# A new order for a fused linear attention and gated MLP kernel, with batch 2's attention output turned by TensorE

## The chip, the cores and the metric

The kernel runs on one core of one Trainium2 chip. The metric is the device time of one execution in microseconds (us), as the median of several runs. The engines are PE (TensorE: matmuls; its weight loads are listed as PEld), DVE (VectorE), ACT (ScalarE), POOL (GpSimd) and SP (SyncE, which here only issues DMAs). Each engine runs its own instructions in the order given, and waits on semaphores where an operand comes from another engine or from a DMA.

## The reference

A linear attention with exponential features, and behind it a gated MLP whose gate mixes the tokens. All inputs are float32, and so is the output (8, 576, 512).

```python
# q, k, v: (8 batches, 8 heads, 576 tokens, 64); w_phi: (64, 128)
def phi(x):
    proj = np.einsum('bhsd,df->bhsf', x, w_phi)
    proj = proj - np.max(np.abs(proj), axis=-1, keepdims=True)
    return np.concatenate([np.exp(proj), np.exp(-proj)], axis=-1)
q_p, k_p = (phi(q), phi(k))
kv = np.einsum('bhsf,bhsd->bhfd', k_p, v)
z = np.sum(k_p, axis=2)
num = np.einsum('bhsf,bhfd->bhsd', q_p, kv)
den = np.einsum('bhsf,bhf->bhs', q_p, z)[..., None] + 1e-06
attn = num / den                       # then heads side by side: x (8, 576, 512)
h = np.maximum(x @ w_in, 0.0)          # w_in: (512, 1024)
u, v = h[..., :512], h[..., 512:]
v_n = (v - mu) / np.sqrt(var + 1e-06)  # over the last axis
v_s = np.einsum('ts,bsd->btd', w_spatial, v_n) + b_spatial[None, :, None]
out = (u * v_s) @ w_out                # w_out: (512, 512)
```

## The kernel before, in words

**Tiles.** A batch has 576 tokens: four chunks of 128 ("main"), and a tail of 64. The tails of two batches share one tile of 128 rows, so there are eight batches (0 to 7) and four tail groups (0 to 3). Work is in bf16, sums in PSUM in float32. PSUM's eight banks are named by hand in each step.

**The order.** Each step is a small function (`@op`). The string ORDER (L17 to L153) lists some 1,500 words, and a loop at the end (L1020) calls one function for each word. A word reads name, arguments, then after a colon the buffer or banks, then after @ the engine where there is a choice: `ckt.1:0@V` is the cast of key tail 1 into buffer 0 on DVE (V; A is ACT, P is POOL, S is SP). The order of the words is the order of the instructions on every engine and DMA queue; nothing reorders them later. The framework puts in the waits that the data and the buffers need.

**The steps of a batch b**, with the names that are used below:
- Loads. `lk`, `lq` load keys and queries with a cast to bf16, issued by POOL (L366, L370); `lv` loads values, `lkt`, `lqt`, `lvt` the tails, issued by SP (L396, L282). Batch 0 is special: its keys come as float32 by SP (`lkf`, L358) and are cast by `ckf`, its queries by `lq0` (L380) on POOL's queue. The weights come on POOL's queue: `lin.0` is w_v, the second half of w_in's columns, `lin.1` is w_u, the first half (L422), `lout` w_out, `lsp` and `lspt` the spatial weights, `lbs` the bias (by SP).
- Turning keys and queries so that the head dimension lies on the partitions: for batches 0 and 1 by PE (`tk`, `tq`, four 128x128 transposes each, L496, with a copy from PSUM `tkc`, `tqc`), for the others by DMA transposes issued by SP (`xk`, `xq`, L482). Tails: cast `ckt`, `cqt`, turned by PE (`tkt`, `tqt`, L524, copies `tktc`, `tqtc`).
- Keys: projection `kp` (L548), maxima `km` (DVE, L553, 1.2 us each), two exponentials `ke` (ACT, L557), the maxima's exponentials `kem`; `vs` scales the values (mostly POOL, L606), `kv` sums over the tokens (L637, L639), `kvc` copies. Tails the same with a t: `kpt`, `kmt`, `ket`, `vst`.
- Queries: `qp`, `qm`, `qs` (split of the maxima), `qt` and `qc` (turned by PE and copied), `qf` (features with the maxima subtracted, L664, L668), `qe` (ACT, L673), `qn` (L720), `qr` and `qx` (division, DVE). Tails again with a t.
- Turning the attention output x: for batches 0, 1 and 7 by PE, `tx` (four transposes, L803) with the copy `txc`; for the others by two DMA transposes `xx` issued by SP (L796). The tails of groups 1 and 2 by the DMA transpose `xxt` (L815), the others by PE (`txt`, L822).
- MLP: `vm` (L835), `vr` (relu), `vb`, `va`, `vx` (DVE statistics), `vw`, `vy`, `vn` (POOL, normalizing), `um` (L931), `ur` (relu), `spt`/`spc` (the spatial weights turned), `sm` (L946, L948), `sg` (gate, DVE), `om` (L960), `oc` (copy), `od` (store by SP). Tails: `vmt`, `umt`, `smt`, `sgt`, `omt`, `oct`, `odt`.
- `warm.n.w` issues n matmuls of w columns on a tile of zeros (L349), whose result nobody reads. They fill places where PE would have nothing to do.

The batches overlap: while one batch is in its MLP, the next ones are at their keys and queries. Buffers are few (3 for `ld`, 7 for the turned T, 4 for v, 2 for the tails' `tf`, 3 for xT), so a load or a transpose can be issued only when the reader of the buffer's last content is through.

Of the kernel before, what the change touches and what calls it, by code (L numbers as in the profile page):

```python
# [33 lines left out]
tkc.1.0.0:4@V kv.0.2:2 qe.0.0.1.0:3 vst.0.1.1@V qet.0.1 kv.0.3:3 qn.0.0.0:0,1 qr.0.0.0:0 qe.0.0.1.1 qf.0.1.1:4,5
kvc.0.2@A kvc.0.3@V qe.0.1.1.0:4 qe.0.1.1.1 qx.0.0.0:0 qn.0.1.0:6,7 lq.2:1 qr.0.1.0:1 qnt.0.0:2,3 qx.0.1.0:1 qrt.0.0:2
qn.0.0.1:0,1 lvt.1:0@S qxt.0.0:0 qr.0.0.1:0 tk.1.0.1:6 spt.4:7 kp.1.0:4,5 tkc.1.0.1@V qn.0.1.1:2,3 qx.0.0.1
warm.1.512:6 warm.1.128:6 tx.0.1:6 tx.0.0:0 spc.4@A ke.1.0.0:4 qr.0.1.1:1 qx.0.1.1 txt.0.0:1 txc.0.0:0@A txtc.0.0:0@V
# [5 lines left out]
va.0.1 kp.1.2:4,5 ur.0.0:1@A ke.1.2.0:1 vs.1.0.0:0@P qp.1.0.1:0,1 vsz.1.1@P vxt.0.0 vx.0.0 spt.3:3 qm.1.0.0:1 vb.0.2:3
qm.1.0.1:2 ke.1.2.1 vs.1.0.1@P um.0.3:2 vwt.0.0:0 kp.1.3:6,7 um.0.1:0 vb.0.3:0 ur.0.3@A va.0.2:2 xk.2.0:3 vw.0.0:1
va.0.3 ke.1.3.0:2 ke.1.3.1 vsz.1.0@P lv.2.0:1@S kv.1.0:1 spc.3@V um.0.2:2 vx.0.1 lout spt.2:3 km.1.2:3 kvc.1.0:1@A
qp.1.1.0:4,5 qs.1.0.0:2@P km.1.3:0 warm.2.128:3 spt.0:1 vy.0.0 warm.5.128:1 qt.1.0.0:6 qs.1.0.1:0@P vyt.0.0 spc.2@A
ur.0.1@A kem.1.3:2 qt.1.0.1:0 kv.1.1:3 tkt.1:7 qm.1.1.0:3 vw.0.1:2 vn.0.0:1@P qp.1.1.1:4,5 qc.1.0.1:1@V vy.0.1
qc.1.0.0:0@V vnt.0.0:0@P vn.0.1@P spc.0@A kvc.1.1@V vn.0.3@P vn.0.2@P lk.3:0 xk.2.1:4 qm.1.1.1:0 vs.1.3.0:2@P
qf.1.0.0:0,1 qs.1.1.0:1@P vs.1.3.1@P cqt.1:0@A warm.2.128:3 sm.0.2:3 sm.0.3:6 qe.1.0.0.0:1 ur.0.2@A qe.1.0.0.1
qf.1.0.1:4,5 kem.1.2:3 sg.0.2 qp.2.1.0:2,3 qp.2.0.0:0,1 vsz.1.3@P tktc.1:0@A sg.0.3 lv.3.1:2@S qm.2.1.0:1 sm.0.0:6  # L50
sm.0.1:7 qt.1.1.0:2 vs.1.2.0:3@P qm.2.0.0:2 qe.1.0.1.0:0 qs.1.1.1:2@P lkt.2:0@S vsz.1.2@P vs.1.2.1@P qc.1.1.0:2@V
qt.1.1.1:3 qe.1.0.1.1 xk.3.0:5 sg.0.1 qc.1.1.1:0@V kv.1.3:4 qn.1.0.0:0,1 sg.0.0 kvc.1.3@A qr.1.0.0:2 kv.1.2:2
qx.1.0.0:2 qf.1.1.0:4,5 qp.2.0.1:6,7 kvc.1.2@A qnt.0.1:2,3 qe.1.1.0.0:3 qn.1.0.1:0,1 qm.2.0.1:3 qrt.0.1:0 warm.2.128:1
qf.1.1.1:6,7 qxt.0.1 qr.1.0.1:1 qe.1.1.0.1 warm.2.128:1 txt.0.1:2 qx.1.0.1 txtc.0.1@V qp.2.1.1:4,5 lq.3:1 qe.1.1.1.0:4
qm.2.1.1:0 xk.3.1:2 om.0.3:3 qn.1.1.0:0,1 qe.1.1.1.1 tx.1.0:2 qn.1.1.1:6,7 oc.0.3:0@A xq.3.0:0 qr.1.1.0:2 qx.1.1.0:0
tx.1.1:3 kpt.1:4,5 qr.1.1.1:0 qx.1.1.1 kp.2.0:0,1 txc.1.0:1@A txc.1.1@A ke.2.0.0:3 vmt.0.1:2 qs.2.0.1:0@P kmt.1:1
vrt.0.1:0@A vm.1.0:3 ket.1.0:0 tx.1.3:2 km.2.0:2 tx.1.2:6 vm.1.1:7 txc.1.3@V vm.1.3:2 vr.1.0:1@A qs.2.1.0:1@P
kem.2.0:0 vbt.0.1:2 txc.1.2@V qt.2.1.0:3 vr.1.1:2@V qs.2.0.0:2@P om.0.0:6 vat.0.1:3 vxt.0.1 ket.1.1 lk.4:2 ke.2.0.1
tqt.1:7 vs.2.0.0:0@P vr.1.3:4@A tqtc.1:0@A vb.1.0:1 kp.2.1:4,5 kp.2.2:0,1 va.1.0:4 vm.1.2:2 qc.2.1.0:1@V vs.2.0.1@P
vb.1.1:3 ke.2.1.0:4 umt.0:3 kemt.1:1 va.1.1 vwt.0.1:3 vr.1.2:3@A om.0.2:7 oc.0.0:1@A vb.1.3:0 vx.1.0 um.1.0:2  # L60
urt.0:0@A km.2.1:0 qt.2.0.0:3 km.2.2:3 vb.1.2:2 va.1.2:5 um.1.2:6 qc.2.0.0:2@V va.1.3 ke.2.1.1 kem.2.1:2 qf.2.1.0:4,5
vyt.0.1 um.1.3:3 vx.1.1 oc.0.2:2@A ke.2.2.0:0 ur.1.0:2@V qe.2.1.0.0:1 kem.2.2:3 xq.3.1:3 qt.2.0.1:2 om.0.1:7 ur.1.2@V
smt.0.0:6 vnt.0.1@P vw.1.0:4 qs.2.1.1:1@P qc.2.0.1:0@V ur.1.3@V vy.1.0 oc.0.1:3@V qe.2.1.0.1 sgt.0.0 vn.1.0:2@P
kp.2.3:2,3 ke.2.2.1 vs.2.1.0:1@P qf.2.0.0:4,5 kp.3.0:6,7 qt.2.1.1:0 vw.1.1:0 vn.1.1@P vy.1.1 km.2.3:2 vst.1.0.0:0@P
um.1.1:1 qc.2.1.1:1@V vn.1.3@P vn.1.2@P qe.2.0.0.0:2 od.0.2@S sm.1.2:0 vs.2.1.1@P lv.3.0:3@S qe.2.0.0.1 km.3.0:1
xk.4.0:4 od.0.3@S ur.1.1@A qp.3.0.0:4,5 lv.4.1:1@S lq.5:0 smt.0.1:1 ke.2.3.0:2 sg.1.2 sm.1.0:0 qm.3.0.0:3 vsz.2.0@P
sgt.0.1 ke.2.3.1 vst.1.0.1@P qp.3.0.1:4,5 od.0.0@S ke.3.0.0:1 sm.1.1:1 vstz.1@P sg.1.0 vs.2.2.0:2@P vsz.2.1@P
kem.2.3:0 ke.3.0.1 qf.2.0.1:2,3 qs.3.0.0:2@P qe.2.0.1.0:0 qm.3.0.1:1 qpt.1:4,5 sg.1.1 qmt.1:2 kp.3.1:6,7 sm.1.3:0
vs.2.3.0:3@P xk.4.1:6 qe.2.0.1.1 kv.2.0:1 vs.2.2.1@P kv.2.1:4 km.3.1:0 omt.0:5 sg.1.3 ckt.2:0@A ke.3.1.0:3 kem.3.1:2
kvc.2.0:2@V vsz.2.2@P vs.2.3.1@P oct.0:4@A vst.1.1.1@P kp.3.3:2,3 kvc.2.1@V km.3.3:3 ke.3.1.1 qp.3.1.1:0,1 vsz.2.3@P  # L70
kv.2.2:4 kv.2.3:5 kvc.2.2@A qm.3.1.1:0 kem.3.0:3 qn.2.0.0:6,7 kvc.2.3@A qr.2.0.0:1 ke.3.3.0:4 qx.2.0.0:1 warm.1.128:4
qn.2.0.1:4,5 od.0.1@S om.1.3:0 qr.2.0.1:2 qf.2.1.1:6,7 vst.1.1.0@P kem.3.3:0 qx.2.0.1 qp.3.1.0:4,5 ke.3.3.1 qm.3.1.0:3
# [983 lines left out]
```

## Time and profile before

| | |
|---|---|
| median of 3 runs | 266.23 us (264.95 to 268.85) |
| the profiled execution | 265.98 us, of which its span is 264.2 us |
| granted TensorE clock | 0.999 |
| PE's matmuls on zeros (L349) | 19.1 us busy |
| DMA | 41.91 MB, 159 GB/s on average |
| queue of SP and queue of POOL | 56.3% and 29.0% of 16 engines' span |
| keys, queries: issue to landing (median) | 7.8 and 8.9 us |
| values: least, median, most | 4.2, 7.3, 18.3 us |
| DMA transposes T<-ld (24), xT<-x (10), xTt<-xt (2), median | 5.5, 4.4 and 5.2 us |

How to read it: the span is the time from the first to the last instruction in the profile, and what is predicted is the device time. Busy time of an engine is the sum over its instructions; matmuls overlap in the pipeline, so their spacing in a row is shorter than the duration of one. An idle time is put down to what ended it. A share of the DMA above 1 in a stretch means that the transfers' packets overlap.

The first PE work on data starts 4.1 us into the span (`tk.0.0.0`), the first `kv` at 24.5, the first `vm` at 36.5, the first `um` at 44.6, the first `om` at 65.9 us. The last `kv` runs to 221 us; from there on only the MLPs of batches 5 to 7 and the last queries are left. The last matmul starts at 259.6 us; the last copy and store end the span.

### The profile page before, as it was taken

How to read it: one execution, taken by the hardware profiler on the slowest of the kernel's cores; microseconds unless marked ns; L12 is line 12 of the kernel's file. 1: busy time of each engine (PE TensorE's matmuls, PEld its weight loads, DVE VectorE, ACT ScalarE, POOL GpSimd, SP SyncE). 2: the span in 40 equal slices, each digit the busy share in tenths (PEclk: the TensorE clock that was granted, in tenths of full speed). 3: DMA queues.
4: the chain of work that ended last, by engine and by line, in shares of the span. 5: the costliest groups of instructions: out<-in, count | busy, mean ns of one | idle time of the engine just before them, and what ended most of it. 6: DMA issues, size and time to landing. Idle time of an engine off the chain costs nothing.

```text
span 264.2 us, 8269 instructions
## 1 busy us (share of the span) xinstructions
PE 249.1 (94%) x3305; PEld 152.4 (58%) x3342; DVE 219.8 (83%) x438; ACT 203.7 (77%) x338; POOL 164.1 (62%) x297
## 2 busy tenths in 40 slices
...
GB/s 150 219 204 252 204 221 230 194 238 179 166 61 194 181 120 125 157 175 182 227 159 246 275 90 180 141 178 188 201 78 2 123 122 2 0 110 51 122 186 213
DMA packets 82075, 41.91 MB, mean 159 GB/s; under 512 B 50994, under 2 KB 77298, under 8 KB 82036
## 3 DMA queue, kind: packets, MB, share of 16 engines
q1 hardware_dynamic: 64612, 31.28, 56.3%
q0 software_dynamic: 17424, 10.10, 29.0%
...
## 4 chain that ended last, share of the span: by engine, by line
PE 69%; DVE 11%; DMA 7%; issue 4%; POOL 3%; SPq 2%; ACT 2%; POOLq 0%; ACTq 0%; DVEq 0%
PE banks L946 9%; PE banks L960 9%; PE banks L931 8%; PE banks L835 8%; PE banks L637 6%; PE banks L548 5%; PE banks L720 5%; DMA xT<-x 3%; PE banks L664 3%; DMA xTt<-xt 2%; DVE mq L553 2%; PE banks L349 2%; PE banks L948 2%; PE banks L668 2%; DMA ob<-in_k_dram 2%
## 5 line engine op out<-in xcount | busy, mean ns | idle before, releaser
L673 ACT ACTIVATE qf<-banks 128x1024 bf16<-128x1024 f32 x72 | 70.4, 1033 | 4.9 <-PE banks L668 4.6
L606 POOL TENSOR_TENSOR vs<-v,em 128x512 bf16<-128x512 f32 x59 | 60.8, 1040 | 20.7 <-ACT em L563 7.6
L557 ACT ACTIVATE kf<-banks 128x1024 bf16<-128x1024 f32 x64 | 64.7, 1036 | 3.3 <-PE banks L548 2.1
L553 DVE TENSOR_REDUCE mq<-banks 128x8 f32<-128x1024 f32 x36 | 43.4, 1216 | 2.3 <-PE banks L548 1.9
L553 DVE TENSOR_REDUCE mk<-banks 128x8 f32<-128x1024 f32 x36 | 43.4, 1214 | 1.8 <-PE banks L548 1.1
L844 POOL TENSOR_TENSOR rs<-mv,neghalf 128x2 f32<-128x2 f32 (+2 forms) x21 | 13.9, 664 | 32.2 <-DVE mv L841 26.4
L835 PE MATMUL banks<-w_v,xT 128*128 128x512 bf16 x116 | 30.7, 380 | 2.7 <-DMA xT<-x 2.1
L946 PE MATMUL banks<-w_spT,vn 128*128 128x512 bf16 x121 | 32.1, 380 | 0.5 <-issue 0.2
L931 PE MATMUL banks<-xT,w_u 128*128 128x512 bf16 x128 | 32.3, 380 | 0.0
L960 PE MATMUL banks<-w_out,uT 128*128 128x512 bf16 x116 | 30.9, 380 | 0.8 <-issue 0.2
L548 PE MATMUL banks<-wphi,T 64*128 64x128 bf16 x512 | 24.3, 218 | 1.6 <-DVE T L268 1.1
L850 POOL TENSOR_SCALAR vn<-vr,rs,mv 128x512 bf16<-128x512 bf16 x31 | 23.5, 764 | 0.7
L637 PE MATMUL banks<-vs,kf 128*128 128x66 bf16 x512 | 23.8, 194 | 0.0
L637 PEld LDWEIGHTS <-kf 128*128 128x128 bf16 x512 | 21.8, 98 | 3.3 <-issue 0.5
L955 DVE TENSOR_TENSOR uT<-banks,uT 128x512 bf16<-128x512 f32 x32 | 21.2, 679 | 2.6 <-PE banks L948 1.8
L733 DVE TENSOR_TENSOR x<-banks,rc 128x512 bf16<-128x512 f32 x32 | 21.9, 686 | 1.1 <-PE banks L349 0.4
L862 DVE BATCH_NORM_STATS2 st<-vr 128x6 f32<-128x512 bf16 x32 | 21.6, 677 | 0.9 <-ACT vr L272 0.8
L548 PEld LDWEIGHTS <-T 64*128 64x128 bf16 x512 | 15.7, 94 | 10.7 <-issue 7.8
L272 ACT ACTIVATE vr<-banks 128x512 bf16<-128x512 f32 (+1 forms) x26 | 15.7, 605 | 7.9 <-PE banks L835 4.8
L349 PE MATMUL banks<-blank 128*128 128x128 bf16 (+1 forms) x96 | 19.1, 315 | 2.6 <-DVE blank L344 1.2
L720 PE MATMUL banks<-kv,qf 128*128 128x66 bf16 x512 | 21.1, 194 | 0.0
L639 PE MATMUL banks<-vst,kft 128*128 128x66 bf16 x128 | 21.0, 192 | 0.0
...
## 6 DMA issues: line engine op xcount, KB each, us to landing
...
```

Of the source, the lines that this page charges most:

```text
L349: nc.tensor.matmul(out=bank(place)[:, 512 - w:512], lhsT=blank[:, 0:P], rhs=blank[:, 0:w], start=True, stop=True)
L548: nc.tensor.matmul(out=bank(banks[y])[:, n * F:(n + 1) * F], lhsT=xT[halves[y], n, :], rhs=wphi[halves[y], :], start=True, stop=True)
L553: nc.vector.tensor_reduce(out=out_, in_=pp.rearrange("p y (n f) -> p y n f", f=F), axis=AX.X, op=ALU.max, apply_absolute_value=True)
L557: nc.scalar.activation(out=kf[:, s].rearrange("p y n f -> p y (n f)"), in_=pp, func=AF.Exp, bias=0.0, scale=(1.0, -1.0)[s])
L606: ENG[e].tensor_tensor(out=at["vs", (b, j)][:, s, :, 0:D], in0=at["v", (b, j // 2)][:, (j % 2) * n:(j % 2 + 1) * n, :], in1=at["em", (b, j ...
L637: nc.tensor.matmul(out=pv[:, hh, s, :], lhsT=kf[:, s, c % 2, 2 * hh + c // 2, :], rhs=w[:, s, NB * hh + c, :], start=(c == 0), stop=False)
L673: nc.scalar.activation(out=at["qf", u][:, s].rearrange("p y n t -> p y (n t)"), in_=at["pq", u], func=AF.Exp, bias=0.0, scale=(1.0, -1.0)[s])
L720: nc.tensor.matmul(out=at["pn", u][:, y, n, :], lhsT=f[:, s, y, n, :], rhs=at["kv", b][:, hg * HH + n, s, :], start=(s == 0), stop=(s == 1))
L835: nc.tensor.matmul(out=bank(place)[r], lhsT=lhs[:, kc, r], rhs=w_v[:, kc, :], start=(kc == 0), stop=(kc == KC - 1))
L931: nc.tensor.matmul(out=bank(place).rearrange("p (c t) -> p c t", c=NB), lhsT=w_u[:, kc, dc * P:(dc + 1) * P], rhs=at["xT", b][:, :, kc, :] ...
L946: nc.tensor.matmul(out=bank(place), lhsT=at["vn", b][:, c, cs], rhs=w_spT[:, c, 0:T0], start=(c == 0), stop=False)
L960: nc.tensor.matmul(out=bank(place), lhsT=at["uT", b][:, dc, c * P:(c + 1) * P], rhs=w_out[:, dc, :], start=(dc == 0), stop=(dc == KC - 1))
```

## The change

Only ORDER changes; every function stays as it is.

- `xx.2.0` and `xx.2.1` go; `tx.2.0` to `tx.2.3` and `txc.2.0` to `txc.2.3` come in (16 transposes on PE, three copies on DVE, one on ACT).
- `lin.0` stands behind `lk.1` (the second batch's keys) and `lsp` in POOL's queue; `lspt` is POOL's first word, and `lq.1` and `lin.1` come much earlier. On SP the loads `lkf.3`, `lv.3.0`, `lqt.3` come earlier, `lv.1.0`, `lv.2.1`, `lkt.3` later.
- Nearly all other words stand in another place, and some change engine: `ckf` from two on ACT, one each on POOL and DVE to three on POOL, one on DVE; `ckt` from three on DVE, one on ACT to two on POOL, one each on ACT and DVE; `cqt` from one to three of four on POOL; `tkc` from five to seven of eight on DVE; `ur` from 20 to 26 of 32 on ACT; `vr` from 22 to 18 of 32 on ACT; `kvc` from 14 to 16 and `oc` from 16 to 14 of 32 on DVE; `vn` from 31 to 29 on POOL, the others on DVE.
- The matmuls on zeros go from 49 of 512 columns and 51 of 128 columns to 39 and 32.

The diff replaces the whole string; here are its start and the lines that hold the words spoken of.

```diff
-zblank@V zmhl.2@V zmhl.1@V zmhl.0@V lkf.0:0,0@S cident csel chalf@P ckf.0@A lphi@S zvnt.1@A zvnt.0@V warm.8.512:0
-tk.0.0.0:0 zsp@V lkf.1:1@S lkf.2:2@S cphi@V ckf.1@P warm.4.512:1 warm.2.128:1 tk.0.0.1:1 lkt.0:0@S tkc.0.0.0:0@A
-tkc.0.0.1@V ckf.2@A lq0.0.4:1 warm.3.512:0 kp.0.1:2,3 tk.0.1.0:0 km.0.1:0 tkc.0.1.0:1@A ckt.0:0@V lq0.4.4 kp.0.0:4,5
-lqt.0:1@S csel2@V ke.0.0.0:0 warm.2.512:1 warm.1.128:1 kp.0.2:6,7 lkf.3:3@S km.0.2:1 kem.0.1:0 ke.0.0.1 ckf.3@V
-lv.0.0:0@S km.0.0:2 warm.1.512:0 warm.3.128:0 tkt.0:0 tktc.0:0@A ke.0.1.0:1 lin.0 cqt.0:0@P warm.7.512:1 warm.1.128:1
-tk.0.1.1:0 warm.4.512:1 kpt.0:4,5 ke.0.1.1 tqt.0:1 kem.0.2:1 zvst.0@V ke.0.2.0:2 warm.2.512:2 warm.1.128:2 tq.0.0.1:2
-tq.0.0.0:3 kmt.0:3 tkc.0.1.1@V tqc.0.0.0:2@A tqtc.0:0@V tqc.0.0.1@V warm.1.512:0 warm.1.128:0 qpt.0:0,1 ke.0.2.1
-qmt.0:0 warm.1.512:3 qp.0.1.0:2,3 kem.0.0:2 ket.0.0:0 lk.1:2 qm.0.1.0:1 warm.2.512:6 warm.1.128:6 tq.0.1.1:6
-tq.0.1.0:7 kp.0.3:0,1 kemt.0:3 tqc.0.1.0:3@V qs.0.1.0:0@V lspt:4 lsp:0 vs.0.1.0:0@P ket.0.1 qst.0:1@P lvt.0:0@S
+lkf.0:0,0@S zblank@V lphi@S lkf.1:1@S lkf.2:2@S lspt:3 cident zmhl.1@V zvnt.0@A ckf.1@P ckf.0@V zmhl.2@V warm.7.512:0
+warm.2.128:0 tk.0.0.0:0 csel warm.7.512:1 warm.2.128:1 tk.0.0.1:1 lkt.0:0@S zmhl.0@V tkc.0.0.0:0@V zvst.0@V lq0.0.4:1
+lq0.4.4 lk.1:2 zvnt.1@V cphi@V warm.1.512:0 warm.2.128:0 kp.0.0:2,3 km.0.0:0 tkc.0.0.1@V ckt.0:0@P ke.0.0.0:0
+lkf.3:4@S ckf.2@P warm.8.512:0 warm.1.128:0 kp.0.1:4,5 warm.1.512:0 warm.1.128:0 tkt.0:0 kem.0.0:0 lqt.0:1@S
+warm.1.512:1 tk.0.1.0:1 tktc.0:0@A lsp:0 ke.0.0.1 lin.0 ckf.3@P lv.0.0:0@S csel2@V km.0.1:1 tkc.0.1.0:1@V cqt.0:0@P
+warm.1.512:6 warm.2.128:6 kpt.0:6,7 kmt.0:2 kp.0.2:0,1 ke.0.1.0:1 km.0.2:3 ke.0.1.1 kem.0.1:1 warm.3.512:2
+warm.3.128:2 tk.0.1.1:2 warm.1.512:3 tqt.0:3 warm.6.128:2 tq.0.0.0:4 tkc.0.1.1@V lq.1:0 tq.0.0.1:5 tqc.0.0.0:2@V
+tqtc.0:0@A lvt.0:0@S ket.0.0:0 tqc.0.0.1@V qpt.0:2,3 qmt.0:0 warm.1.512:4 warm.2.128:4 qp.0.1.0:4,5 ke.0.2.0:2
+qm.0.1.0:1 ket.0.1 qp.0.0.0:2,3 kp.0.3:6,7 qs.0.1.0:0@P qst.0:1@P tq.0.1.0:4 warm.1.512:5 warm.2.128:5 qt.0.1.0:5
...
-ke.0.3.1 warm.2.512:3 warm.2.128:3 kv.0.0:0 lq.1:0 lv.1.0:2@S lbs:0@S vs.0.2.1@V kem.0.3:2 qe.0.0.0.0:1 qt.0.0.1:1
-qc.0.1.1:2@V warm.2.512:0 warm.1.128:0 tk.1.0.0:0 vs.0.3.1@V qet.0.0:2 vsz.0.3@P lin.1 vst.0.1.0@P kvc.0.1@V
+lin.1 qm.0.0.0:2 ke.0.2.1 tq.0.1.1:0 vs.0.1.0:0@P qs.0.0.0:2@V tqc.0.1.0:3@A tqc.0.1.1@V qc.0.1.0:0@A ke.0.3.0:3
...
-xq.2.1:1 va.0.0:0 vm.0.3:1 vs.1.1.0:1@P warm.1.512:4 tq.1.0.1:6 tq.1.1.1:4 ckt.1:0@V vr.0.2:3@A vat.0.0:1
+kem.1.0:1 kem.1.1:0 spb@P vr.0.1:1@A lk.2:2 chalf@P lout ke.1.0.1 vb.0.0:0 ckt.1:0@P tx.0.3:4 spt.3:2 vr.0.2:2@A
...
-qs.3.0.1:0@P kp.3.2:2,3 xx.2.0:2 om.1.2:1 lq.4:1 qst.1:1@P qt.3.0.0:4 om.1.1:5 km.3.2:2 xq.5.1:5 vs.3.0.0:0@P
-qx.2.1.0:2 qn.2.1.1:4,5 kv.3.0:6 qr.2.1.1:1 kp.4.0:2,3 qx.2.1.1 xx.2.1 vs.3.2.0:3@P vs.3.3.1@P vsz.3.3@P kvc.3.0:0@V
+qe.2.1.1.0:3 om.1.2:7 kem.3.3:0 qe.2.1.1.1 qtt.1:2 km.3.2:0 om.1.1:3 oc.1.3:1@V tx.2.1:6 ke.3.2.1 oc.1.2:4@V
+qf.3.0.0:4,5 qe.3.0.0.0:4 oc.1.1:2@V tx.2.0:7 qn.2.1.0:0,1 qs.3.1.1:0@P od.0.3@S qct.1:2@V qe.3.0.0.1 vs.3.0.1@P
+qs.3.1.0:2@P qn.2.1.1:2,3 txc.2.0:2@V vs.3.3.0:2@P om.1.0:7 vsz.3.0@P qr.2.1.0:0 vst.1.1.0@P txc.2.1@V vs.3.3.1@P
+kv.3.2:1 kvc.3.2@A kem.4.0:1 tx.2.3:2 qf.3.1.0:4,5 qe.3.0.1.1 qnt.1.2:0,1 txc.2.3@V va.2.1 qrt.1.2:2 xq.4.0:0
+qxt.1.2:0 qn.3.0.0:2,3 qn.3.0.1:6,7 qr.3.0.0:0 vm.2.3:0 qx.3.0.0:1 tx.2.2:1 qe.3.1.0.0:0 vx.2.0 xxt.1:1 qe.3.1.0.1
+qr.3.0.1:1 txc.2.2@A qx.3.0.1 xx.3.0:0 qf.3.1.1:2,3 kp.4.1:4,5 lk.5:2 qn.3.1.0:6,7 vm.2.2:1 qe.3.1.1.0:3 vr.2.3:0@V
...
-qr.3.0.0:0 qe.3.0.1.1 qx.3.0.0:0 qt.3.1.1:7 qc.3.1.1:0@V qn.3.0.1:4,5 qe.3.1.0.0:1 vr.2.2:2@A vm.2.3:2 xxt.1:1
-um.3.0:2 od.1.2@S ke.5.0.0:3 va.3.0:3 lvt.2:0@S vr.3.3:1@A lkt.3:0@S sg.2.3 ke.5.0.1 qt.4.0.1:0 vr.3.2:4@V va.3.1
-ke.4.3.0:0 qp.5.1.1:0,1 qs.4.1.1:1@P kem.4.3:3 sg.3.1 qm.5.1.1:2 ckt.3:0@V ke.4.3.1 qf.4.0.0:4,5 qf.4.1.0:6,7 sm.3.2:2
+qx.4.1.0:1 kp.5.3:0,1 qe.5.0.1.0:3 lk.7:2 qmt.2:3 om.3.0:4 om.3.3:5 qe.5.0.1.1 lkt.3:1@S km.5.3:0 ckt.3:0@V qt.5.1.0:2
```

237 lines of the change are left out of this document (118 added, 119 removed).

## The prediction, made before the changed kernel was run

> **What bounds the kernel now.** I read the page's busy shares first, then a table of busy time by stretches of 8 us (busy us and instruction count of PE, PEld, DVE, ACT, POOL; granted clock; DMA share; GB/s), then the same table for the fill matmuls of L349 alone, and last the timelines around PE's waits.
>
> ```profile
> PE 249.1 (94%) x3305; PEld 152.4 (58%) x3342; DVE 219.8 (83%) x438; ACT 203.7 (77%) x338; POOL 164.1 (62%) x297
> ```
>
> ```profile
> 0.00:8.00 8.00, 6.47 (x41) 2.88 (x43) 3.00 (x12) 4.05 (x7) 3.15 (x11) 1.00 0.65 165
> 8.00:16.00 8.00, 6.77 (x69) 3.58 (x68) 7.22 (x11) 6.83 (x13) 3.71 (x6) 1.00 1.15 209
> 16.00:24.00 8.00, 7.67 (x107) 4.68 (x108) 7.52 (x10) 7.19 (x14) 6.00 (x13) 1.00 1.25 235
> ...
> 40.00:48.00 8.00, 6.85 (x75) 3.85 (x73) 7.78 (x18) 7.05 (x12) 6.45 (x13) 1.00 1.28 206
> ...
> 104.00:112.00 8.00, 6.10 (x133) 4.40 (x128) 4.62 (x9) 6.14 (x9) 4.76 (x10) 1.00 1.09 157
> 112.00:120.00 8.00, 6.93 (x105) 4.07 (x101) 7.51 (x22) 7.32 (x9) 1.13 (x4) 1.00 1.40 175
> ...
> 128.00:136.00 8.00, 7.95 (x51) 3.70 (x51) 7.97 (x16) 4.91 (x11) 5.35 (x12) 1.00 0.98 172
> ...
> 256.00:264.00 8.00, 3.90 (x18) 1.56 (x16) 0.05 (x1) 3.17 (x6) 0.00 (x0) 0.99 0.53 199
> ```
>
> And the fills alone (PE busy, PEld busy, clock, DMA):
>
> ```profile
> 0.00:8.00 8.00, 5.46 (x17) 1.81 (x17) 1.00 0.65 165
> 8.00:16.00 8.00, 4.82 (x23) 2.01 (x24) 1.00 1.15 209
> 16.00:24.00 8.00, 4.26 (x28) 2.04 (x29) 1.00 1.25 235
> ```
>
> PE is 94% busy, but 14.5 us of its first 24 us are fills: of 20.9 us busy there only 6.4 us is work, and the start is set by loads and by DVE. From 24 to 120 us PE stands idle 6.1 us (8.00 less its busy time, stretch by stretch); after 120 us nearly nothing until the last output leaves. So what is saved ahead of 120 us reaches the end, if DVE allows it: it too is 97 to 99% busy in several stretches. PE's timeline shows where the idle time lies:
>
> ```profile
> 44.27 0.40 PE L548 MATMUL banks<-wphi,T 64*128 64x128 bf16 x8 [1.15 <-DVE T L268]
> ...
> 106.31 0.81 PE L835 MATMUL banks<-w_v,xT 128*128 128x512 bf16 x3 [1.90 <-DMA xT<-x]
> ...
> 119.93 1.04 PE L835 MATMUL banks<-w_v,xTt 128*128 128x512 bf16 x3 [0.98 <-DMA xTt<-xt]
> ```
>
> **Batch 2 turned by PE.** Gone are two DMA transposes (xx.2.0, xx.2.1) and the 1.90 us for which vm.2.0 waited on the first, which took 8.0 us to land. Added are 16 transposes; eight of L803 stand in a row as 0.61 us, so 16 cost 1.2 us of PE. The four copies (three on DVE at 0.42, one on ACT at 0.59) lie where DVE has 3.4 us free (104 to 112 us); without that cover they cost DVE 1.2 us. Net -0.7; bounds -0.7 and, if the next transposes are late instead, +1.2.
>
> **The tail's transpose.** xxt.1 cost 0.98 us: it took 6.5 us to land. Between its source qxt.1.2 and its reader vmt.1.2 the changed order puts one um (0.86) and one qn (0.51) more, two groups of four transposes more (0.3 each) and one qf less (0.5): about 1.2 us more of cover. I take -0.98; bounds -0.98 and 0. For xxt.2 the cover falls by one um, from about 5.0 to 4.2 us of PE work, against 3.8 us to land: 0, at worst +0.8.
>
> **The cast ckt.1.** The 1.15 us before 44.27 trace back to DVE, where one cast took four times its usual time while POOL multiplied:
>
> ```profile
> 42.07 1.75 DVE L268 CAST tl<-tf 128x512 bf16<-128x512 f32 x1
> ```
>
> ```profile
> 42.49 1.04 POOL L606 TENSOR_TENSOR vs<-v,em 128x512 bf16<-128x512 f32 x1
> ```
>
> The cast of the same shape at 147.30 us, with POOL empty, took 0.42 us. The change puts ckt.1 on POOL (0.61 us there), in front of two vs multiplications that have slack. -1.15; bounds -1.15 and 0. The Trainium skill (SBUF — State Buffer, "SBUF: two separate sides") says that POOL and a DVE cast in a two-port mode share a port pair by an exclusive lock, whoever starts second waiting it out; the row agrees. By that rule ckt.3, still on DVE and now among POOL's vs, could pay the same 1.33 us, and the sum below would be 1.3 us higher.
>
> **Fills.** Of 512 columns there are 39 for 49, of 128 columns 32 for 51. Eight wide ones in a row take 1.73 us, eight narrow ones 0.62, so 0.216 and 0.078 each. Ahead of kv.0.0 (24.5 us) go 7 wide and 3 narrow (1.75 us), behind it 3 and 16 (1.9 us). A fill that goes is worth something only if no wait takes its place. Behind kv.0.0 I take half, -0.95; bounds -1.9 and 0.
>
> **The start.** Casts move to POOL: there ckf.1 (ends at 6.19), two lq0 issues (0.99, 0.76), lk.1 (0.9), ckt.0 and ckf.2 (0.61 each) now stand in a row, so ckf.2 ends near 10.1 us against 6.83 on ACT, and tk.0.1.0 waits for it. In return kp.0.0 and kpt.0 go first, and DVE clears the vst and vnt blocks earlier. The queries' load still lands at 14.5 us (PE waited for it there), the first values at 15.4. I take 0; bounds -1.75 (the fills) and +1.2 (one DVE maximum later).
>
> **Weights and loads.** lin.0 moves behind lk.1 and lsp in POOL's DMA queue, lq.1 and lin.1 forward from 25 us to some 13 us. Before, w_v landed at 20.1 us and was read at 36.5; the spatial weights, last of the queue's first loads, landed at 29.7. Now w_v comes last of the same loads, so near 29.7: about 6 us of cover are left, and I cost it at 0. Beyond 6 us late, each us costs one. On SP, lkt.3 now comes closer to ckt.3 (11.6 us of PE work instead of 15 us); its kind lands in 6.8 us (median), 15.3 at most: 0, at worst +3.7, with all of DVE's queue behind the cast.
>
> **DVE's share.** Ahead of om.2.3 (136 us) DVE has 4.1 us more: five more oc (0.68), four txc, two tkc, two tktc, one ur and one qm, less four kvc, two ckt, two txtc, a vr and a vs. ACT has 3.9 us less. DVE stood idle about 11 us between 24 and 136 us, a third of it in the stall at 104 that goes, so most of it fits: +0.6; bounds 0 and +4.1.
>
> Sum: -0.7 - 0.98 - 1.15 - 0.95 + 0.6 = -3.2 us on 264.2, so a span of 261.0. The profiled run took 265.98 us, 1.8 more than its span, and the median of the runs is 0.25 above it: 263.0 us.
>
> **Rivals.** (a) Everything fits: the start gives up its 1.75 us of fills, the rest all 1.9, DVE costs nothing: -6.5, span 257.7, 259.7 us. For it: the fills stand where PE would have idled, and fewer are needed. Against it: DVE, not PE, is full from 8 to 24 us. (b) DVE becomes the bound between 60 and 140 us: PE's gains only turn into waits for DVE, and its extra 4.1 us count in full: span 268.3, 270.3 us. It decides if DVE still idles more than 4 us between 24 and 136 us (11, less 4.1, less the 3.2 forecast): then its extra work no longer fits. For it: 7.97 of 8.00 at 128. Against it: the idle at 104 goes. (c) The loads brought forward, 1.0 MB of lq.1 and lin.1, at 209 to 235 GB/s 4.5 us of transfer, get ahead of the values, which already took up to 14 us to land: 265.5, 267.5 us. Against it: POOL's queue was never empty until 29.7 us anyway. The Trainium skill (DMA: Bandwidth & Descriptors, "Issuing engines are not separate DMA queues") says that loads of SP and POOL interleave on the same 16 engines; the DMA shares above 1.00 agree, and it speaks for (c). (d) The stall moves: the next transposes (xx.3, xxt.1) are late in place of xx.2, and only ckt.1's gain stands against 1.2 us of transposes: 264.2, 266.2 us.
>
> **Numbers.** Forecast 0.36, (a) 0.27, (b) 0.20, (c) 0.10, (d) 0.07. A change under 2% (5.3 us) is about what a measurement of this kernel cannot tell from none. Faster by more, below 260.9: (a) and a quarter of the forecast's spread, 0.36. Slower by more, above 271.6: half of (b), where the cast or a late tail load adds to it, part of (c) and the forecast's upper end: 0.16. The rest 0.48. The range runs from 257.5, (a) with part of PE's unnamed 2 us of idle time, to 270.5, just above (b); the forecast's own is 260 to 266.
>
> **What would show it.** No wait of L835 on xT<-x near 100 us and 16 more transposes of L803; no cast of tl over 0.7 us; vmt.1.2 without a wait; PE's fills in the first 24 us near 12.8 instead of 14.5 us with kv.0.0 near 24.5 us; DVE busy 7.8 or more from 60 to 140 us without PE waiting on it. I am wrong if PE's idle time between 24 and 120 us stays near 6 us, or if POOL waits long for v.

## The result and the profile after

The changed kernel takes 269.04 us (median of 20 runs, 267.77 to 270.36), the kernel before in the same series 266.52 us (20 runs): a ratio of 1.0105, 95% interval 1.0081 to 1.0128. It became slower by 1%, where the forecast had 1.2% faster. Medians here and below are over all runs, while the ratios leave out runs in a slower state that the chip is in at times (three of the twelve of "start freed" below). The profiled execution took 268.97 us with a span of 267.2, against 264.2 before.

From the page after, the busy line and the granted clock in 40 slices:

```profile
PE 248.6 (93%) x3292; PEld 153.0 (57%) x3329; DVE 223.3 (84%) x439; ACT 201.7 (75%) x336; POOL 167.3 (63%) x302
...
PEclk9996899999999999999999999999999999999998
```

DVE has 3.5 us more and ACT 2.0 less than before, in the direction in which the order moved words. New is the clock: the fourth and fifth slice (20 to 33 us) show 6 and 8 tenths. The table by stretches of 8 us of the changed kernel (busy us and count of PE, PEld, DVE, ACT, POOL; granted clock; DMA share; GB/s):

```profile
0.00:8.00 8.00, 6.28 (x29) 2.98 (x29) 3.62 (x12) 2.42 (x3) 3.59 (x9) 1.00 0.68 179
8.00:16.00 8.00, 7.57 (x95) 4.98 (x95) 7.15 (x11) 5.95 (x11) 6.41 (x10) 1.00 1.22 218
16.00:24.00 8.00, 3.56 (x52) 2.17 (x51) 7.93 (x7) 5.78 (x11) 4.50 (x8) 0.90 1.20 222
24.00:32.00 8.00, 7.63 (x121) 5.50 (x121) 7.42 (x15) 6.47 (x12) 4.17 (x11) 0.68 1.29 195
...
104.00:112.00 8.00, 7.90 (x152) 5.58 (x153) 7.56 (x17) 7.59 (x12) 6.70 (x11) 1.00 0.81 105
112.00:120.00 8.00, 7.95 (x170) 5.82 (x168) 7.13 (x19) 7.50 (x13) 2.88 (x6) 1.00 0.85 103
128.00:136.00 8.00, 7.95 (x64) 3.93 (x66) 7.35 (x11) 5.15 (x8) 4.79 (x8) 1.00 1.24 194
```

From 104 to 120 us PE is full where it had been idle for 3 us: what the change was forecast to win there arrived. The largest loss stands in one stretch, 16 to 24 us: PE is busy 3.56 of 8 us (7.67 before), while DVE shows 7.93 with only 7 instructions. From the start of the span to the last matmul, PE's idle time in its timelines is:

| PE idle, us | 0 to 24 | 24 to 120 | behind 120 |
|---|---|---|---|
| before | 3.1 | 6.1 | 1.7 |
| changed | 6.6 | 2.9 | 4.1 |
| changed, `qs.0.0.0` on POOL (below) | 5.1 | 3.1 | 1.9 |

So the 3.2 us less between 24 and 120 us is outweighed by 3.5 us more at the start and 2.4 us more behind 120. The fills of L349 alone, again in stretches of 8 us (PE busy, clock, DMA share, GB/s), are 12.5 us in the first 24, where 14.5 stood before:

```profile
0.00:8.00 8.00, 5.82 (x21) 1.00 0.68 179
8.00:16.00 8.00, 5.26 (x31) 1.00 1.22 218
16.00:24.00 8.00, 1.42 (x9) 0.90 1.20 222
```

The timelines of DVE, POOL and PE in the changed kernel (start, us, engine, line, operation; in brackets the idle time before it and who ended it) say why:

```profile
19.16 0.80 POOL L422 DMA_DIRECT2D w_u<-in_moe_w_in_dram  x1
19.42 3.63 DVE L654 CAST mhl<-mq 128x8 bf16<-128x8 f32 x1
19.98 2.05 POOL L606 TENSOR_TENSOR vs<-v,em 128x512 bf16<-128x512 f32 x2
21.98 1.04 POOL L619 TENSOR_TENSOR vst<-vt,em 64x512 bf16<-64x512 f32 x1
23.17 0.42 DVE L268 COPY T<-banks 128x512 bf16<-128x512 bf16 x1
23.65 0.40 PE L548 MATMUL banks<-wphi,T 64*128 64x128 bf16 x4 [3.26 <-DVE T L268]
...
178.75 1.04 PE L835 MATMUL banks<-w_v,xTt 128*128 128x512 bf16 x3 [1.07 <-DMA xTt<-xt]
```

A cast of 128x8 numbers, `qs.0.0.0`, which the change moved from POOL to DVE, takes 3.63 us; a cast of the same line and shape takes 0.15 at 28.10 us. It starts while POOL issues a DMA and ends when the third POOL multiplication ends that follows without a gap. Behind it in DVE's queue waits the copy `tqc.0.1.1`, and PE waits 3.26 us for that. The first `kv` starts at 29.0 us, not 24.5. (The last line, at 178.75 us, is a wait for a DMA transpose that comes up again below.)

How the lag runs on is estimated from the traces: the time at which PE had done the same amount of listed work (each matmul group at its undisturbed duration, fills left out; the changed kernel has 0.9 us more of it, the 16 transposes, which count from about 110 us on).

| work done, us | 8 | 20 | 76 | 83 | 132 | 160 | 223 |
|---|---|---|---|---|---|---|---|
| before | 25.2 | 39.8 | 100.0 | 109.5 | 160.7 | 189.3 | 252.9 |
| changed | 29.1 | 43.7 | 102.8 | 110.2 | 160.8 | 190.8 | 254.3 |
| changed, qs.0.0.0 on POOL (below) | 25.6 | 40.8 | 99.9 | 107.3 | 157.4 | 187.1 | 250.6 |

So against the kernel before the changed one starts 4 us late, has made good all but about 1 us of that at 160 us (0.1 us by the table and the 0.9 us of transposes), then loses 1.4 us again by 191 us and keeps that lag to 254. Behind its last matmul it loses another 0.8: from there to the end of the span it is 5.0 us, against 4.2 before. Against the same order with `qs.0.0.0` on POOL, the third row, it is 2.9 to 3.7 us late all the way.

### The profile page after: what moved, and what is told of

It reads as the page before. It is cut to its first block, busy times and chain, and to the rows that moved or that the text cites. A ratio compares the mean times of both kernels' runs of the same rounds, so it can differ in the third digit from the quotient of the medians.

```text
span 267.2 us, 8261 instructions
## 1 busy us (share of the span) xinstructions
PE 248.6 (93%) x3292; PEld 153.0 (57%) x3329; DVE 223.3 (84%) x439; ACT 201.7 (75%) x336; POOL 167.3 (63%) x302
## 4 chain that ended last, share of the span: by engine, by line
PE 71%; DVE 13%; DMA 6%; ACT 4%; issue 2%; SPq 1%; POOL 1%; DVEq 0%; ACTq 0%
PE banks L946 10%; PE banks L835 9%; PE banks L931 8%; PE banks L960 8%; PE banks L637 6%; PE banks L548 6%; PE banks L720 4%; PE banks L664 3%; DMA xT<-x 3%; PE banks L948 3%; PE banks L668 2%; DMA xTt<-xt 2%; DVE mq L553 2%; PE banks L349 2%; PE banks L639 1%
## 5 line engine op out<-in xcount | busy, mean ns | idle before, releaser
L606 POOL TENSOR_TENSOR vs<-v,em 128x512 bf16<-128x512 f32 x60 | 61.7, 1040 | 8.0 <-ACT em L563 5.6
L960 PE MATMUL banks<-w_out,uT 128*128 128x512 bf16 x117 | 30.1, 379 | 0.9 <-DVE x L733 0.2
L272 ACT ACTIVATE uT<-banks 128x512 bf16<-128x512 f32 x26 | 15.7, 610 | 11.9 <-PE banks L931 11.8
L548 PEld LDWEIGHTS <-T 64*128 64x128 bf16 x512 | 15.8, 95 | 14.3 <-issue 9.3
L850 POOL TENSOR_SCALAR vn<-vr,rs,mv 128x512 bf16<-128x512 bf16 x29 | 22.0, 767 | 0.8
L720 PEld LDWEIGHTS <-qf 128*128 128x128 bf16 x512 | 18.8, 98 | 3.2 <-issue 0.3
```

The source lines that it names most:

```text
L548: nc.tensor.matmul(out=bank(banks[y])[:, n * F:(n + 1) * F], lhsT=xT[halves[y], n, :], rhs=wphi[halves[y], :], start=True, stop=True)
L606: ENG[e].tensor_tensor(out=at["vs", (b, j)][:, s, :, 0:D], in0=at["v", (b, j // 2)][:, (j % 2) * n:(j % 2 + 1) * n, :], in1=at["em", (b, j ...
L720: nc.tensor.matmul(out=at["pn", u][:, y, n, :], lhsT=f[:, s, y, n, :], rhs=at["kv", b][:, hg * HH + n, s, :], start=(s == 0), stop=(s == 1))
L960: nc.tensor.matmul(out=bank(place), lhsT=at["uT", b][:, dc, c * P:(c + 1) * P], rhs=w_out[:, dc, :], start=(dc == 0), stop=(dc == KC - 1))
```

## The experiments

Theory 1: the cast is kept out while POOL works back to back, and this sets the end. Theory 2: the late start is made good anyway, and the loss comes behind 150 us. Theory 3: it is the place in DVE's queue, not POOL's work. Each ratio is to the kernel before, run on the same chip.

| kernel | median, us | ratio [95%] |
|---|---|---|
| changed, other form of the cast | 268.90 | 1.0105 [1.0059, 1.0151] |
| changed, qs.0.0.0 on POOL | 266.42 | 1.0009 [0.9971, 1.0047] |
| changed, one multiplication in the way, not three | 267.03 | 1.0056 [1.0017, 1.0095] |
| changed, PE's wait filled | 268.83 | 1.0095 [1.0059, 1.0131] |
| qs.0.0.0 on POOL, batch 2 by DMA | 269.69 | 1.0170 [1.0108, 1.0231] |
| qs.0.0.0 on POOL, vmt.2.2 later | 266.77 | 1.0013 [0.9974, 1.0052] |
| that, and ckf.1 on ACT | 271.33 | 1.0213 [1.0155, 1.0271] |
| qs.0.0.0 and ckt.3 on POOL | 265.79 | 0.9986 [0.9950, 1.0022] |
| that, vmt.2.2 later ("late part") | 265.59 | 0.9999 [0.9966, 1.0032] |
| qs.0.0.0 on POOL, start freed | 266.81 | 0.9992 [0.9953, 1.0031] |
| late part and start freed | 267.02 | 1.0046 [1.0011, 1.0080] |
| late part, vm.3 later | 267.65 | 1.0062 [1.0033, 1.0092] |
| before, ckt.1 on POOL | 266.65 | 1.0013 [0.9975, 1.0052] |
| before, batch 2 by PE | 267.10 | 1.0068 [1.0031, 1.0106] |
| before, both of these | 266.68 | 1.0021 [0.9994, 1.0047] |

### The long cast: form, place, and POOL's work

Another form of instruction, in the same place:

```diff
-        ENG[e].tensor_copy(out=m[:, :, 0:HH], in_=mq)
+        if e == "V":
+            nc.vector.tensor_tensor(out=m[:, :, 0:HH], in0=mq, in1=mq, op=ALU.max)
+        else:
+            ENG[e].tensor_copy(out=m[:, :, 0:HH], in_=mq)
```

> The changed kernel, where DVE rounds the maxima to bf16 by a TENSOR_TENSOR (max of mq with itself) instead of a CAST; same place, same queue, same values. Theory 1 (the CAST of qs.0.0.0, 3.63 us at 19.42, was kept out by POOL's back-to-back work; other DVE TENSOR_TENSORs of SBUF ran 0.68 us beside such POOL work): the rounding takes about 0.2 us, PE's wait of 3.26 us at 23.65 is gone, the granted clock of 16 to 32 us is 1.00 again, and the time falls by 3 to 4 us, to about 265.5. Theory 2 (the late start is made good before 125 us anyway, and the loss is in waits after 150 us): the cast and the wait go, but the time falls by less than 1 us, to 268 or more. Theory 3 (the wait is not the cast's own form, but its place in DVE's queue behind data that POOL makes): the rounding still ends near 23 us, no gain.

Nothing changed. DVE's and POOL's timelines of this kernel:

```profile
19.91 3.63 DVE L655 TENSOR_TENSOR mhl<-mq 128x8 bf16<-128x8 f32 x1
...
20.47 2.05 POOL L606 TENSOR_TENSOR vs<-v,em 128x512 bf16<-128x512 f32 x2
22.47 1.03 POOL L619 TENSOR_TENSOR vst<-vt,em 64x512 bf16<-64x512 f32 x1
```

By its letter this is what theory 3 expected. What it refutes is only the belief that a TENSOR_TENSOR goes free: it too ends with POOL's third operation. The Trainium skill (SBUF — State Buffer, "Who interferes with whom") says that a DVE instruction with two inputs in SBUF contends with a GpSimd instruction that reads SBUF; this run agrees, and the expectation had overlooked it. Two runs with the form left alone part theory 1 from 3. First, the operation back on POOL:

```diff
-lin.1 qm.0.0.0:2 ke.0.2.1 tq.0.1.1:0 vs.0.1.0:0@P qs.0.0.0:2@V tqc.0.1.0:3@A
+lin.1 qm.0.0.0:2 ke.0.2.1 tq.0.1.1:0 qs.0.0.0:2@P vs.0.1.0:0@P tqc.0.1.0:3@A
```

> The changed kernel with qs.0.0.0 on POOL, where it was before the change, ahead of vs.0.1.0. Theory 1: the cast starts after POOL's DMA issue near 20.0 us and takes 0.2 us, PE's wait of 3.26 us shrinks to under 0.8, time 265.5 to 266.5. Theory 2: the wait goes, the time stays at 268 or more. Theory 3: as theory 1, since the place is changed too; only the run with the other form parts it from theory 1.

Its timelines of POOL and PE:

```profile
20.57 0.52 POOL L654 CAST mhl<-mq 128x8 bf16<-128x8 f32 x1
...
21.43 0.23 PE L659 MATMUL banks<-ident,mhl 128*128 128x128 bf16 x1 [0.40 <-POOL mhl L655]
```

PE's wait is 0.40 us, the clock is 1.00 throughout, and the time 266.42: 2.6 us less than the changed kernel. Second, the cast stays on DVE, and only POOL's order changes:

```diff
-qf.0.1.0:4,5 vs.0.0.1@P lv.0.1:1@S qct.0:1@A vst.0.0.0:0@P km.0.3:0
+qf.0.1.0:4,5 qs.0.0.1:0@P vs.0.0.1@P lv.0.1:1@S qct.0:1@A vst.0.0.0:0@P km.0.3:0
...
-qs.0.0.1:0@P lbs:0@S vstz.0@P
+lbs:0@S vstz.0@P
```

> The changed kernel with qs.0.0.0 left on DVE, but POOL's qs.0.0.1 (which waits for DVE's next maximum) put ahead of vs.0.0.1 and vst.0.0.0, so that one multiplication of 1.05 us follows POOL's DMA issue in place of three. Theory 1 (the CAST is kept out as long as POOL works back to back): the CAST takes 1.5 to 1.7 us in place of 3.63, PE's wait of 3.26 us becomes 1.1 to 1.4, time 266.5 to 267.5. Theory 3 (it is its place in the order, or a wait for data, and POOL's work has no part): the CAST still takes 3 us or more, no gain.

Its timelines:

```profile
19.96 0.80 POOL L422 DMA_DIRECT2D w_u<-in_moe_w_in_dram  x1
20.23 1.65 DVE L654 CAST mhl<-mq 128x8 bf16<-128x8 f32 x1
20.78 1.05 POOL L606 TENSOR_TENSOR vs<-v,em 128x512 bf16<-128x512 f32 x1
...
22.47 0.29 PE L548 MATMUL banks<-wphi,T 64*128 64x128 bf16 x4 [1.36 <-DVE T L268]
```

One POOL multiplication in place of three, and the cast takes 1.65 us in place of 3.63, the wait 1.36 in place of 3.26: each 2 us, the two operations that were moved away. Theory 1 is shown and theory 3 falls. Theory 2 falls by the run before: without the long cast the time is 2.6 us less, so the start's loss reaches the end. The mended kernel's own first `kv` matmul still starts at 26.44 us, 1.9 us later than before: not all of the late start is the cast.

### The slower clock

```diff
-warm.1.512:1 qtt.0:1 kemt.0:2 vs.0.0.0:1@V warm.2.512:2 warm.1.128:2 qp.0.0.1:2,3
+warm.1.512:1 qtt.0:1 kemt.0:2 vs.0.0.0:1@V warm.14.512:2 warm.1.128:2 qp.0.0.1:2,3
```

> The changed kernel with 12 more fill matmuls of 512 columns (2.6 us) where PE waits 3.26 us for the cast; cast and wait for it stay. If the granted clock of 0.90 and 0.68 in 16 to 32 us comes from PE's standing idle, it is 1.00 here, and the pairs of L664 after 24 us take 0.39 us again, not 0.61. If that slower clock costs time, the run is 0.5 to 1.5 us faster than the changed kernel (267.5 to 268.5); if DVE sets the pace there, or the loss is made good later, it is the same within 0.3 us.

Its table by stretches:

```profile
16.00:24.00 8.00, 6.64 (x72) 4.08 (x72) 7.29 (x6) 5.88 (x11) 4.05 (x8) 1.00 1.21 222
24.00:32.00 8.00, 6.11 (x114) 4.34 (x113) 7.86 (x16) 5.80 (x12) 3.76 (x10) 1.00 1.28 193
```

The clock is full, the pairs of L664 take 0.39 us again, and the time is 268.83, the same. The slow clock came from PE's standing idle and cost nothing that these runs can tell (the intervals are 0.5 to 0.7% wide): DVE, at 7.86 of 8, sets the pace there.

### The prediction's steps alone, in the kernel before

```diff
-tq.1.0.1:6 tq.1.1.1:4 ckt.1:0@V vr.0.2:3@A vat.0.0:1
+tq.1.0.1:6 tq.1.1.1:4 ckt.1:0@P vr.0.2:3@A vat.0.0:1
```

> The kernel before, with ckt.1 alone moved from DVE to POOL. The prediction's step: the 1.75 us cast on DVE and PE's 1.15 us wait at 44.27 go, the time falls by up to 1.15 us. Rival: the cast now stands among POOL's vs multiplications and delays vn or v, or the gain is lost in the later wait of 1.90 us for xT<-x: under 0.3 us of gain.

No gain, though the waits of 1.15 us at 44.27 and of 1.90 us at 106.31 are both gone from PE's timeline. There is a larger one instead:

```profile
120.19 1.04 PE L835 MATMUL banks<-w_v,xTt 128*128 128x512 bf16 x4 [2.38 <-DMA xTt<-xt]
```

It was 0.98 at 119.93. The tail's transpose was issued 1.1 us sooner (112.22 us, 113.35 before) but took 7.9 us to land in place of 6.5, so it landed near 120 us in both, and what was won ahead of it was lost there. Why it took longer is not shown. Then batch 2 by PE in the kernel before, alone and with that cast:

```diff
-qs.3.0.1:0@P kp.3.2:2,3 xx.2.0:2 om.1.2:1
+qs.3.0.1:0@P kp.3.2:2,3 om.1.2:1
...
+vs.3.0.1@P tx.2.0:7 oc.1.2:0@A ke.3.2.0:0 kem.3.2:1 tx.2.1:1 txc.2.0:2@V
+qtt.1:4 txc.2.1@A oc.1.1:1@V
...
-qx.2.1.1 xx.2.1 vs.3.2.0:3@P
+qx.2.1.1 tx.2.2:7 vs.3.2.0:3@P
...
+xq.5.0:1 tx.2.3:1 txc.2.2@V vsz.3.1@P qet.1.0:2 qt.3.0.1:6 txc.2.3@A vm.2.0:7
```

> The kernel before, with batch 2 alone turned by PE: 16 transposes and four copies (two on DVE, two on ACT) in place of two DMA transposes; all else as before. The prediction's steps: -0.70 for xx.2 and, because the SP queue is freer, -0.98 for xxt.1: 264.9 against 266.6. If the start and the cast of ckt.1 set the pace and the 1.90 us was hidden anyway: no gain. If the gap in the changed kernel (3.3 us between the two ways of turning) holds here too: 263.5.

> The kernel above with ckt.1 also on POOL, which alone gave nothing because vmt.1.2 then waited 2.38 us. With the SP queue freer, the cast's 1.15 us should now reach the end: 0.8 to 1.2 us less than the kernel above. If vmt.1.2 still waits for xTt near 120 us: the same as the kernel above.

Alone it is slower, 1.0068. PE's timeline of that run has no wait for a transpose any more, but two for the copies that came in:

```profile
106.21 0.37 PE L664 MATMUL banks<-T,wphi 64*128 64x512 bf16 x1 [1.10 <-ACT xT L266]
110.24 1.02 PE L835 MATMUL banks<-w_v,xT 128*128 128x512 bf16 x4 [0.58 <-DVE xT L268]
```

1.10 + 0.58 + 1.2 us of transposes is 2.88 us, and 1.90 + 0.98 = 2.88 went: nothing is left. Why the median is even higher is open; the profiled execution alone (267.5 us of span) can't tell, since its first keys were cast late (PE waits 2.20 us for them at 13.56, 0.47 at 11.95 before). That wait changes from one execution to the next: with the same start it is 1.67 us in the trace with ckt.1 on POOL and 2.54 us in the trace with both edits. With the cast on POOL as well the wait of 1.15 us is gone and the median falls by 0.4 us, half of what was expected and less than the intervals of the two ratios can tell from nothing.

### Batch 2 by DMA in the mended kernel

```diff
-qx.2.0.1 ke.3.3.1 ckt.2:0@A
+qx.2.0.1 xx.2.0:2 ke.3.3.1 ckt.2:0@A
...
-qx.2.1.1 qet.1.0:1
+qx.2.1.1 xx.2.1 qet.1.0:1
```

(`tx.2.0` to `tx.2.3` and their copies are taken out.)

> The changed kernel with qs.0.0.0 on POOL, and batch 2 turned by two DMA transposes again in place of 16 on PE and four copies. The prediction's step (-1.90 +1.2) makes it 0.7 us slower than the same kernel with PE's transposes (266.42), plus the wait for xTt, which it put at 0.98: 267.1 to 268.1. Rival 1 (the SP queue's transposes are what sets 97 to 120 us, as the wait of 2.38 us for xTt in the kernel before with ckt.1 moved suggests): vmt.1.2 waits 2 us or more and starts near 120 us as in both kernels before, and what the start won is lost: 268 or more. Rival 2 (the transposes on PE cost what they save): 266.0 to 266.6.

```profile
111.19 0.61 PE L548 MATMUL banks<-wphi,T 64*128 64x128 bf16 x8 [3.48 <-DMA T<-ld]
```

3.3 us slower than with PE's transposes (the medians are of two chips; the ratios, 1.0170 and 1.0009, differ by 1.6%, or 4 us, and the first rests on six runs), more than the 1.7 us of the prediction's two terms. Neither of the two waits of the prediction comes back. The long wait, the line of PE's timeline above, is neither for xT nor for xTt but for turned keys or queries: `xk.4.1`, `xq.5.1` and `xq.5.0` stand behind `xx.2.1` in SP's queue, which waits for x until 103.8 us, and are issued at 105.6, 106.9 and 109.3 us, where the mended kernel issued them at 89.8, 91.6 and 97.7. PE's wait ends at 111.19, when the second of them has landed (111.14). So in this place a DMA transpose cost what queued behind it; the run does not part that from the transfers' own time.

### Behind 125 us, and the start

```diff
-um.4.2:6 va.4.2:1 ur.4.0:2@A vw.4.0:0 vmt.2.2:7 vy.4.0 qe.5.1.1.1
-ur.4.2@A kp.6.3:0,1 ... vn.4.0:2@P vrt.2.2:3@A um.4.3:6 xk.7.0:6
+um.4.2:6 va.4.2:1 ur.4.0:2@A vw.4.0:0 vy.4.0 qe.5.1.1.1
+ur.4.2@A kp.6.3:0,1 ... vn.4.0:2@P um.4.3:6 vmt.2.2:7 vrt.2.2:3@A xk.7.0:6
```

> The changed kernel with qs.0.0.0 on POOL, and vmt.2.2 moved behind kp.6.3, qp.6.1.0 and um.4.3 (about 1.8 us of PE work more while xxt.2 lands). If the 0.88 us that PE waits there at 175 us sets the end: wait gone and 0.6 to 0.9 us faster than 266.42. If DVE or ACT wait next (vrt.2.2 comes later): no gain.

The wait for xTt is gone, the time is not less. In this run PE waited 0.90 us for xT at 123 us, and 0.35 for ACT's vr at 182.69. Then `ckt.3:0@V` becomes `ckt.3:0@P`, without and with that edit:

> The changed kernel with qs.0.0.0 on POOL, and ckt.3 on POOL too. On DVE ckt.3 took 0.99 us beside POOL's vs, 0.42 without, and PE waited 0.40 us behind it at 158 us (the prediction left up to 1.33 us of it out of its sum). If that wait reaches the end: 0.4 us less than 266.42, near the edge of what five rounds tell; the cast of 0.99 us and the wait for mT are gone from the trace. If the wait only moves to vm or vmt of the last batches: no gain.

> The changed kernel with qs.0.0.0 on POOL, ckt.3 on POOL and vmt.2.2 moved back together. If the two waits (0.40 and 0.88 us) are what takes back the lead behind 125 us: 265.2 to 265.6, and no wait of PE over 0.3 us between 130 and 250 us. If PE only waits for something else there (ACT's vr after the moved vmt.2.2): 266.0 or more.

Without it, the 0.99 us cast and PE's 0.40 us behind it are gone, but xTt is waited for 1.39 us in place of 0.88. With both, the waits over 0.25 us that are left from 100 us on in PE's timeline are two:

```profile
122.70 1.90 PE L835 MATMUL banks<-w_v,xT 128*128 128x512 bf16 x8 [0.95 <-DMA xT<-x]
...
181.33 1.02 PE L835 MATMUL banks<-w_v,xT 128*128 128x512 bf16 x4 [0.35 <-ACT vr L272]
```

265.59 us is 0.8 less than with qs.0.0.0 alone by the medians, but at a ratio of 0.9999 to the kernel before: equal to it. The wait for xT, whose transpose was issued 8 us earlier, was tried next (`umt.1:0` and `qp.4.1.0` ahead of `vm.3.0` and `vm.3.1`):

> The kernel with qs.0.0.0 and ckt.3 on POOL and vmt.2.2 moved back (aq_end, 265.59), with umt.1 and qp.4.1.0 also put ahead of vm.3.0 and vm.3.1 (1.05 and 0.31 us of PE work). If the wait of 0.95 us for xT<-x at 122.7 us reaches the end: 264.6 to 264.9, and no wait for xT there. If ACT, which now turns uT for umt before vr, makes vm.3.1 wait in its place, or nothing is gained because DVE is late next: 265.3 or more.

```profile
124.80 1.02 PE L835 MATMUL banks<-w_v,xT 128*128 128x512 bf16 x4 [1.45 <-ACT uTt L272]
```

The wait for the DMA became a longer one for ACT, and the kernel slower. At the start, two edits. `ckf.1:@P` to `ckf.1@A`, on top of the vmt.2.2 edit:

> The kernel above, and ckf.1 cast on ACT in place of POOL, where it took 1.44 us beside DVE's memset and copies of SBUF (0.61 us in the kernel before). If the first keys set the start, PE's 0.74 us wait at 6.85 us goes and the time falls by another 0.3 to 0.7 us; if the queries' load (landing near 15.3 us) sets the start, nothing changes.

```profile
2.53 1.56 POOL L380 DMA_DIRECT2D ld<-in_q_dram  x2
...
15.07 0.61 POOL L268 CAST tl<-tf 128x512 bf16<-128x512 f32 x1 [10.09 <-DMA tf<-in_k_dram]
...
15.74 0.61 PE L524 MATMUL banks<-ident,tl 128*128 128x128 bf16 x4 [4.50 <-POOL tl L268]
```

The slowest kernel of all. With the cast gone from POOL's queue, the queries of batch 0 are issued at 2.53 us, not 6.99 as with the vmt.2.2 edit alone, and the keys of batch 1 behind them at 4.07, not 8.54. The key tail, issued on SP at 3.6 us in both, is cast at 15.07, not 9.42. The cast had held back two loads that now got ahead of the key tail; which of the two delayed it is not parted. Last, the cast stays on POOL but its neighbours on DVE go:

```diff
-zvnt.0@A ckf.1@P ckf.0@V ... tkc.0.0.0:0@V zvst.0@V lq0.0.4:1 lq0.4.4 lk.1:2 zvnt.1@V cphi@V
+zvnt.0@A zvnt.1@A ckf.1@P zvst.0@V ckf.0@V ... tkc.0.0.0:0@V lq0.0.4:1 lq0.4.4 lk.1:2 cphi@V
...
-qs.0.0.0:2@P vs.0.1.0:0@P
+qs.0.0.0:2@P
...
-vsz.0.0@P kem.0.2:3
+vsz.0.0@P vs.0.1.0:0@P kem.0.2:3
...
-qc.0.0.1:0@V kv.0.1:5 qf.0.0.1:6,7 kvc.0.0:0@V qc.0.1.1:1@A kvc.0.1@V
+qc.0.0.1:0@V qf.0.0.1:6,7 kvc.0.0:0@V qc.0.1.1:1@A kv.0.1:5 kvc.0.1@V
```

> The changed kernel with qs.0.0.0 on POOL; the clears of vst (DVE, 0.94 us) moved ahead of the first cast and that of vnt to ACT, so that ckf.1 on POOL no longer stands beside them; vs.0.1.0 (1.05 us on POOL, needed only by kv.0.1) behind what kv.0.0 needs, and kv.0.1 behind qf.0.0.1. If the port that POOL and DVE share is what still costs there: ckf.1 takes 0.6 us in place of 1.44, the wait of 0.99 us for vs goes, 1.0 to 1.8 us less than 266.42. If the loads set the start, the queries issued sooner land no sooner, or the keys behind them land later: no gain, or a loss as in the kernel with ckf.1 on ACT (271.3).

> Both of these together. If both gains are real and add up: 264 to 265, below the kernel before by 0.5 to 1%. If what is won at the start is lost in the transposes that land near 123 us (xT<-x waited 0.68 to 0.90 us there in three runs): the same as the better of the two.

`ckf.1` takes 0.61 us in place of 1.24 (1.44 in the changed kernel) and the wait of 0.99 us for POOL's vs is gone, as expected. The time is not less (ratio 0.9992 against 1.0009). With the late part as well, PE waits 1.08 us for xT at 122.85 us, and what the start had won is gone early: the 13th `qe` on ACT starts at 57.4 us with and without the freed start. Why the median is 1.4 us higher than the late part's alone, on the same chip, is open.

## Why the prediction was wrong, step by step

**The step that failed is "The start ... I take 0; bounds -1.75 (the fills) and +1.2".** It followed the first keys' casts and the loads, and did not look at what else the order moved between POOL and DVE. `qs.0.0.0` went from POOL to DVE, into a place where POOL issues a DMA and then does three operations without a gap. The cost was a wait of PE of 3.26 us, nearly three times the upper bound, a first `kv` 4.5 us late (of which 1.9 stay without the cast), and 2.6 us at the end. The mechanism stood in the prediction itself, at `ckt.1` (1.75 us beside POOL's vs) and as a risk for `ckt.3`; it was applied to two casts of 512 columns and not to the small ones, whose own time is 0.15 us. It would have had to be asked of every word that the diff moves to DVE. The price was misread too. The prediction took it for one POOL multiplication, the one at 42.49 us. POOL's timeline of the kernel before has two lines ahead of it:

```profile
41.33 1.06 POOL L606 TENSOR_TENSOR vs<-v,em 128x512 bf16<-128x512 f32 x1
42.33 0.21 POOL L268 CAST vs<-em 128x32 bf16<-128x32 f32 x1
```

The cast of 42.07 us began while the first of these ran and ended at 43.82, behind all three. "Whoever starts second" explains the first of the three, not the two that started behind the cast: the length of POOL's chain counted, as it did for `qs.0.0.0`.

**A second step failed: "what is saved ahead of 120 us reaches the end, if DVE allows it".** With `qs.0.0.0` on POOL the trace is 3.3 us ahead at 132 us of work, 2.4 when the 0.9 us of added transposes are taken off, against 3.2 forecast for the span. At 223 us of work 1.4 of that is left (2.3 less 0.9): PE has waited 0.88 us for xTt and 0.40 for mT in between. Behind the last matmul 0.8 more goes (5.0 us to the end of the span, 4.2 before), and the span is 0.6 us shorter. By the medians nothing is left (ratio 1.0009): this execution (265.34 us) was the fastest of its ten, 1.1 us under their median, and that of the kernel before 0.5 us under its own. Taking the two waits away did not bring a gain that the runs can tell either (0.9999), so what holds the end in the mended kernel stays open.

The prediction's own sign of being wrong, PE's idle time from 24 to 120 us staying near 6 us, did not come: it fell to 2.9. The loss lay on both sides of the stretch that the sign watched. And a change of 1% could be told from none, which the prediction had doubted below 2%.

**Fills: -0.95.** In the first 24 us 2.0 us of them went (12.8 forecast, 12.5 seen), and waits took their place: PE's idle time there rose by 3.5 us, by 2.0 with `qs.0.0.0` on POOL. The term itself was for the fills behind the first `kv`. There they went from 4.6 us busy to 2.5, and no run shows what that was worth alone.

**The cast ckt.1: -1.15.** The wait went in every kernel with the cast on POOL. Alone in the kernel before it is worth nothing (ratio 1.0013); in its trace the tail's transpose landed no sooner and PE waited 2.38 us for it. That is what rival (d) says of a stall that moves, here for this edit alone. With batch 2 turned by PE the cast made 0.4 us by the medians, which the runs do not tell from nothing.

**Batch 2 by PE: -0.7, and xxt.1: -0.98.** Right in sign in the changed order, but by another wait than the two that were named: 3.3 us there, most of it for keys or queries that stood in SP's queue behind the transpose. In the kernel before it is worth nothing with the copies where they were put. The bound of +1.2 "if the next transposes are late instead" covered that, but with the wrong wait: the copies were late. In the changed kernel one of the next transposes was late too: PE waits 0.68 us for batch 3's xT at 125.15 us.

**xxt.2: 0, at worst +0.8.** It was 1.07 us late, 0.88 in the mended kernel. **ckt.3 on DVE**, named in the prediction with 1.3 us and left out of the sum: the cast took 0.99 us, so 0.57 more than alone, and PE waited 0.40 us behind it.

**DVE's +0.6.** PE waits 0.53 and 0.38 us for DVE between 81 and 86 us and 0.40 at 162 (that one is ckt.3): about the size. The time of rival (b), 270.3 us, is the nearest to the measured one, by chance: its mechanism did not come. DVE idled 7.8 us between 24 and 136 us (11.3 before), so its 3.5 us more fitted in. By the test in the prediction, idle time over 4 us, (b) would have come; the test does not part the two. **Weights and loads: 0.** No wait for a weight. Rival (c) did not come either: the values landed in 6.0 us (median), 7.3 before. The kernel with ckf.1 on ACT shows the like of it with other loads (4.50 us), as soon as nothing holds the queries' load back.
